# Holding the second DMA ring and the DMA transposes behind DVE writes, and reordering the first key products, at the head of a gated attention and MLP kernel

## The chip, the cores and the metric

The kernel runs on one core of one Trainium2 chip. The metric is the device time of one execution in microseconds (us). A run counts as slow when it is over 1.5% above the fastest run of the same kernel. The span of a profile is about 1.8 us shorter than the measured time.

PE is the matrix engine, DVE the vector engine, ACT the scalar engine, POOL the general engine, and SP the engine that issues most DMAs. PEld in a profile is PE's loading of weights. A DMA is a transfer from memory; a ring is the queue of DMA commands of the engine that issues them (here SP or ACT); a load lands when its last part has arrived.

## The reference

```python
def ref(A_x, A_wqkv, A_wo, B_w1, B_b1, B_w2, B_b2, gate_w):      # cut
    x = A_x                                    # 1 x 2048 x 512, bf16
    g = sigmoid((x * gate_w).sum(-1, keepdims=True))
    q, k, v = split_heads(x @ A_wqkv)          # 32 heads of 16
    phi = lambda t: where(t > 0, t + 1, exp(t)) + 1e-6
    kv  = einsum("bhsd,bhse->bhde", phi(k), v)
    z   = einsum("bhsd->bhd", phi(k))
    a   = normalized(phi(q) @ kv, phi(q) @ z) @ A_wo
    h   = layernorm(x)
    b   = (gelu(h^T @ B_w1 + B_b1) @ B_w2 + B_b2)^T
    return g * a + (1 - g) * b
```

Only the key stage matters here: k = x Wk, phi(k), the Gram product x^T phi(k), and the statistics of the layer norm, which run on DVE beside it.

## The kernel before

x is cut into 16 tiles of 128 rows. Wk has four chunks of 128 rows, Wk0 to Wk3. A key product of a tile takes four matmuls, one per chunk, and needs x transposed. Tiles 0 to 3 are transposed on PE and copied out by DVE or ACT. Tiles 4 to 15 come transposed by DMA.

```python
    load_x(nc.sync, 0, 1)                       # eight first loads of 128 KB
    load_x(nc.scalar, 1, 1)                     # on two rings: SP (sync), ACT (scalar)
    load_wk(nc.sync, 0)
    load_x(nc.scalar, 2, 1)
    load_x(nc.sync, 3, 1)
    for k, q in ((1, nc.scalar), (2, nc.sync), (3, nc.scalar)):
        load_wk(q, k)
    load_xT(4, 2)                               # DMA transposes, two tiles each
    load_xT(6, 2)
    load_x(nc.sync, 4, 4)
    # ... cut: the other loads, memsets ...
    warm_up(6)                                  # six matmuls on constants
    # ... cut ...
    transpose_tile(0, False)                    # PE transposes; copy on DVE
    transpose_tile(1, True)                     # copy on ACT
    transpose_tile(2, False)
    ln_step(0)                                  # statistics on DVE
    for k in range(2):
        for t in range(HEADS - 1):
            k_part(t, (k,))                     # chunks 0 and 1 of tiles 0, 1, 2
    transpose_tile(HEADS - 1, True)             # tile 3, copy on ACT
    ln_step(1)
    for t in range(HEADS):
        k_part(t, range(2 if t < HEADS - 1 else 0, ND))
        k_phi(t)                                # exp on ACT, two instructions on DVE
    for t in range(HEADS, NT):                  # steady state
        k_part(t, range(ND))
        k_phi(t)
        g_tile(t - LAG)                         # Gram product, four tiles behind
        if t > LAG:
            ln_step(t - LN_LAG)
        # ... cut ...
```

Of the kernel before, what the change touches and what calls it, by code (L numbers as in the profile page):

```python
# [10 lines left out]
BF16 = mybir.dt.bfloat16  # L11
# [4 lines left out]
def kernel(  # L16
# [13 lines left out]
    nc = tc.nc  # L30
    P = nc.NUM_PARTITIONS
# [6 lines left out]
    S, D = X.shape  # L38
    F = B_w1.shape[1]
    NT = S // P  # L40
    ND = D // P
# [4 lines left out]
    FB = 4  # L46
# [4 lines left out]
    w1_chunks = [(j, min(FB, NF - j)) for j in range(0, NF, FB)]  # L51
# [3 lines left out]
    wqkv_view = A_wqkv.rearrange("(k p) n -> p k n", p=P)  # L55
    wo_view = A_wo.rearrange("(j p) n -> p j n", p=P)
    w1_view = B_w1.rearrange("(t p) f -> p t f", p=P)
# [3 lines left out]
    wpool = ctx.enter_context(tc.tile_pool(name="wstream", bufs=4))  # L61
# [5 lines left out]
    def keep(shape, dtype, name):  # L67
        return persist.tile(shape, dtype, name=name, tag=name)

    def bank(name, dtype=FP32):  # L70
        return ps.tile([P, SC], dtype, name=name, tag="bank")

    xs = keep([P, NT, D], BF16, "xs")
    hs = keep([P, NT, D], BF16, "hs")
    xT = keep([P, ND, S], BF16, "xT")
    wq_sb = keep([P, ND, D], BF16, "wq_sb")
    wk_sb = keep([P, ND, D], BF16, "wk_sb")
    wv_sb = keep([P, ND, D], BF16, "wv_sb")
    wo_sb = keep([P, ND, D], BF16, "wo_sb")
# [32 lines left out]
    def mm(o, lhsT, rhs, start, stop, **kw):  # L112
        nc.tensor.matmul(o, lhsT=lhsT, rhs=rhs, start=start, stop=stop, **kw)  # L113
# [14 lines left out]
    def load_x(q, t0, n):  # L128
        q.dma_start(out=xs[:, t0 : t0 + n, :], in_=x_view[:, t0 : t0 + n, :])

    def load_wk(q, k):
        q.dma_start(out=wk_sb[:, k, :], in_=wqkv_view[:, k, D : 2 * D])

    def load_xT(t0, n):
        nc.sync.dma_start(
            out=xT[:, :, t0 * P : (t0 + n) * P], in_=X[t0 * P : (t0 + n) * P, :], transpose=True
        )

    load_x(nc.sync, 0, 1)
    load_x(nc.scalar, 1, 1)  # L140
    load_wk(nc.sync, 0)
    load_x(nc.scalar, 2, 1)
    load_x(nc.sync, 3, 1)
    for k, q in ((1, nc.scalar), (2, nc.sync), (3, nc.scalar)):
        load_wk(q, k)
    load_xT(4, 2)
    load_xT(6, 2)
    load_x(nc.sync, 4, 4)
    for t0, n in ((8, 4), (12, 4)):
        load_xT(t0, n)  # L150
        load_x(nc.sync, t0, n)
    nc.sync.dma_start(out=wq_sb[:], in_=wqkv_view[:, :, 0:D])
    w1c = []
    for c, (j0, nb) in enumerate(w1_chunks):
        w = wpool.tile([P, NT, FB * P], BF16, name="w1c", tag="wc")
        w1c.append(w)
        for t0 in range(0, NT, 8) if c == 0 else (0,):
            t1 = t0 + 8 if c == 0 else NT
            nc.sync.dma_start(
                out=w[:, t0:t1, : nb * P], in_=w1_view[:, t0:t1, j0 * P : (j0 + nb) * P]  # L160
            )
        if c == 0:
            nc.sync.dma_start(out=wv_sb[:], in_=wqkv_view[:, :, 2 * D : 3 * D])
            nc.sync.dma_start(out=wo_sb[:], in_=wo_view)

    nc.vector.memset(ones_f[:], 1.0)
    nc.vector.memset(mhalf[:], -0.5)
    nc.vector.memset(Z32[:], 0.0)
    nc.gpsimd.memset(ident[:], 0.0)
    nc.gpsimd.affine_select(  # L170
        out=ident[:], in_=ident[:], compare_op=ALU.not_equal, fill=1.0, base=0,
# [5 lines left out]
        out=maskQ[:], in_=maskH[:].rearrange("p (a m) -> p m a", m=2), op=ALU.max, axis=AX.X  # L177
# [12 lines left out]
    def warm_up(n, cols=SC):  # L190
        for _ in range(n):
            mm(wps[:, :cols], warm[:, 0:P], warm[:, :cols], True, True)

    act_warm = keep([P, 1], FP32, "act_warm")
    nc.scalar.activation(out=act_warm[:], in_=ones_f[:], func=ACT.Exp)
    warm_up(6)

    def transpose_tile(t, on_act):
        pt = bank("pt", BF16)
        for k in range(ND):  # L200
            nc.tensor.transpose(pt[:, k * P : (k + 1) * P], xs[:, t, k * P : (k + 1) * P], ident[:])  # L201
        dst = xT[:, :, t * P : (t + 1) * P]
        src = pt[:].rearrange("p (k s) -> p k s", k=ND)
        if on_act:
            nc.scalar.activation(out=dst, in_=src, func=ACT.Copy)  # L205
        else:
            nc.vector.tensor_copy(out=dst, in_=src)

    def phi(dst, acc):
        e = work.tile([P, SC], BF16, name="e", tag="e", bufs=6)  # L210
        nc.scalar.activation(out=e[:], in_=acc[:], func=ACT.Exp)  # L211
        nc.vector.tensor_scalar(  # L212
            out=e[:], in0=e[:], scalar1=1.0, scalar2=PHI_EPS, op0=ALU.min, op1=ALU.add
        )
        nc.vector.scalar_tensor_tensor(  # L215
            out=dst, in0=acc[:], scalar=0.0, in1=e[:], op0=ALU.max, op1=ALU.add
        )
# [3 lines left out]
    def k_part(t, ks):  # L221
        if t not in kaccs:
            kaccs[t] = bank("kacc")
        for k in ks:
            mm(
                kaccs[t][:], xT[:, k, t * P : (t + 1) * P], wk_sb[:, k, :],
                k == 0, k == ND - 1,
            )

    def k_phi(t):  # L230
        phi(pk[:, t, :], kaccs.pop(t))
# [46 lines left out]
    def ln_step(u):  # L278
        ln_stats(u)
        if u % TPC == TPC - 1:  # L280
            ln_rstd(u // TPC)

    HEADS = 4
    transpose_tile(0, False)
    transpose_tile(1, True)
    transpose_tile(2, False)
    ln_step(0)
    for k in range(2):
        for t in range(HEADS - 1):
            k_part(t, (k,))  # L290
    transpose_tile(HEADS - 1, True)
    ln_step(1)
    for t in range(HEADS):
        k_part(t, range(2 if t < HEADS - 1 else 0, ND))
        k_phi(t)
    LAG = 4
    LN_LAG = 3
# [156 lines left out]
    for j in range(NB0, NF):  # L454
        c, jj = divmod(j, FB)
# [18 lines left out]
        out=gg[:], in0=gth[:], scalar1=0.5, scalar2=0.5, op0=ALU.mult, op1=ALU.add  # L474
    )
    nc.vector.tensor_scalar(
        out=c1[:], in0=gth[:], scalar1=-0.5, scalar2=0.5, op0=ALU.mult, op1=ALU.add
# [3 lines left out]
    for t in range(NT):  # L481
        c, tl = divmod(t, TPC)
        aps = bank("aps")
        for j in range(ND):
# [3 lines left out]
            out=a_sc[:], in_=aps[:], func=ACT.Identity,  # L488
            scale=gg[:, t : t + 1], bias=c2[:, t : t + 1],
        )  # L490
        for c0, W in ((0, D - P), (D - P, P)) if t == NT - 1 else ((0, D),):
            cs = slice(c0, c0 + W)
            yps = bank("yps")
            for f in range(NF):
# [6 lines left out]
                out=ot[:, :W], in0=yps[:, :W], scalar=c1[:, t : t + 1], in1=a_sc[:, cs],  # L501
# [35 lines left out]
```

## Time and profile before

| | before |
|---|---|
| time, first three runs | 164.32 us median (164.17 to 164.72) |
| span of the profile | 162.5 us |
| PE busy | 158.1 us, 97% |
| first key product / tile 4's first key product | 4.82 / 9.00 us |

The first view is the page of the kernel before: its span, the busy times of the engines, and the chain of work that ended last.

```profile
span 162.5 us, 2183 instructions
...
PE 158.1 (97%) x823; PEld 72.8 (45%) x837; DVE 89.5 (55%) x210; ACT 63.3 (39%) x97; POOL 17.5 (11%) x34
...
PE 97%; issue 0%; DVE 0%
```

PE is busy nearly from end to end, so only the few places where it waits can give time back. The timeline of PE shows where they are. Its columns are the start, the busy time, engine, line, operation, the tiles and their shapes, the count, and in brackets the idle time before with what ended it.

```profile
2.08 1.48 PE L113 MATMUL wps<-const-bfloat16-1.0 128*128 128x512 bf16 x3
3.55 1.47 PE L201 MATMUL pt<-ident,xs 128*128 128x128 bf16 x12
4.82 1.97 PE L113 MATMUL kacc<-wk_sb,xT 128*128 128x512 bf16 x6
6.62 0.39 PE L201 MATMUL pt<-ident,xs 128*128 128x128 bf16 x4
6.84 3.19 PE L113 MATMUL kacc<-wk_sb,xT 128*128 128x512 bf16 x14
9.86 1.03 PE L113 MATMUL gacc<-pk,xs 128*128 128x512 bf16 x4
```

A row merges instructions of one group. The rows overlap a little because the record of one such matmul lasts 0.38 us (its end is modelled), while the next one starts 0.216 us after it. The six key products (kacc) from 4.82 take until 6.62: three with Wk0, then three with Wk1, which start at 5.97. From 6.62 on the stream is dense: 10 products for tiles 0 to 3, four for tile 4 from 9.00.

ACT's timeline in the same kernel shows the order of the copies (xT) and the exps (e):

```profile
4.62 0.60 ACT L205 ACTIVATE xT<-pt 128x512 bf16<-128x512 bf16 x1 [0.42 <-PE pt L201]
7.04 0.60 ACT L205 ACTIVATE xT<-pt 128x512 bf16<-128x512 bf16 x1 [1.82 <-PE pt L201]
7.54 2.26 ACT L211 ACTIVATE e<-kacc 128x512 bf16<-128x512 f32 x4
```

The copy of tile 3 runs at 7.04, ahead of the exps, and PE wants its result only at 8.14.

### The profile page before, as it was taken

The numbers are of one execution on the slowest core, as the hardware profiler recorded it, in microseconds if no ns is written. First come the engines' busy times: TensorE is split into PE (matmuls) and PEld (weight loads), VectorE is DVE, ScalarE is ACT, GpSimd is POOL, SyncE is SP. The second block draws the span as 40 slices with busy tenths as digits, with TensorE's granted clock in tenths as the row PEclk, the third lists the DMA queues.
The fourth block names the chain that finished last, engine by engine and source line by source line (L and its number), as shares of the span: only waits on it lengthen the run. The fifth ranks groups of instructions, "written<-read, shape, count | busy, mean of one in ns | idle before, by whom it ended". The sixth has DMA issues, their size and how long they took to land.

```text
span 162.5 us, 2183 instructions
## 1 busy us (share of the span) xinstructions
PE 158.1 (97%) x823; PEld 72.8 (45%) x837; DVE 89.5 (55%) x210; ACT 63.3 (39%) x97; POOL 17.5 (11%) x34
## 2 busy tenths in 40 slices
PE   7999999999999999999999999999999999999993
PEld 3544444444444444444444444444444444444452
DVE  0599999967999999519995301166211111111112
ACT  3463386648667483212865113111122222111110
POOL 3000711200110000001415500050000000000000
PEclk9999999999999999999999999999999999999999
DMA  5999999999900006600892699822000001110001
GB/s 152 239 212 237 280 316 334 379 386 387 338 12 0 0 0 221 230 4 0 280 318 80 197 325 297 315 99 102 32 32 32 32 32 41 48 44 33 32 32 32
DMA packets 30057, 25.05 MB, mean 154 GB/s; under 512 B 7968, under 2 KB 29472, under 8 KB 30048
## 3 DMA queue, kind: packets, MB, share of 16 engines
q1 hardware_dynamic: 27744, 21.76, 43.4%
q0 software_dynamic: 1440, 2.38, 5.8%
q10 hardware_dynamic: 864, 0.79, 1.4%
q8 instruction: 6, 0.10, 0.3%
q14 instruction: 3, 0.02, 0.0%
HBM read 21.11 MB, written 2.23 MB: 144 GB/s over the span
## 4 chain that ended last, share of the span: by engine, by line
PE 97%; issue 0%; DVE 0%
PE uacc L113 30%; PE yps L113 30%; PE kacc L113 9%; PE aps L113 8%; PE gacc L113 8%; PE qacc L113 8%; PE wps L113 2%; PE pt L201 1%; PE denps L113 1%; PE kvps L113 0%; PE w2ps L113 0%; DVE ot L500 0%; PE pt L330 0%
## 5 line engine op out<-in xcount | busy, mean ns | idle before, releaser
L113 PE MATMUL uacc<-hs,w1c 128*128 128x512 bf16 x219 | 51.0, 379 | 0.4
L113 PE MATMUL yps<-uT,w2c 128*128 128x512 bf16 (+2 forms) x234 | 50.6, 366 | 0.2
L500 DVE SCALAR_TENSOR_TENSOR ot<-yps,c,a_sc 128x512 bf16<-128x512 f32 (+2 forms) x17 | 12.2, 720 | 45.2 <-PE yps L113 42.0
L113 PEld LDWEIGHTS <-w2c 128*128 128x128 bf16 x238 | 22.8, 98 | 25.9
L113 PEld LDWEIGHTS <-w1c 128*128 128x128 bf16 x224 | 21.8, 98 | 26.3 <-issue 0.2
L487 ACT ACTIVATE a_sc<-aps,c,gg 128x512 f32<-128x512 f32 x16 | 12.4, 777 | 46.7 <-PE aps L113 39.6
L324 ACT ACTIVATE uT<-uacc,bcol 128x512 bf16<-128x512 f32 x14 | 9.3, 688 | 21.7 <-PE uacc L113 21.7
L113 PE MATMUL aps<-W2sb,pqT 128*128 128x512 bf16 x63 | 16.2, 379 | 0.1
L113 PE MATMUL kacc<-wk_sb,xT 128*128 128x512 bf16 x63 | 16.2, 385 | 0.0
L113 PE MATMUL qacc<-xT,wq_sb 128*128 128x512 bf16 x63 | 16.2, 379 | 0.0
L113 PE MATMUL gacc<-pk,xs 128*128 128x512 bf16 x62 | 15.5, 379 | 0.1
L251 ACT ACTIVATE hs<-xs,nmr,rstd 128x512 bf16<-128x512 bf16 x16 | 12.8, 805 | 1.9 <-DVE nmr L245 1.9
L211 ACT ACTIVATE e<-qacc 128x512 bf16<-128x512 f32 x16 | 9.6, 597 | 9.2 <-PE qacc L113 8.3
L211 ACT ACTIVATE e<-kacc 128x512 bf16<-128x512 f32 x16 | 9.3, 595 | 6.9 <-PE kacc L113 5.6
L439 POOL DMA_DIRECT2D rex<-rd_dram x16 | 9.5, 602 | 22.9 <-DVE pqT L441 20.5
L215 DVE SCALAR_TENSOR_TENSOR pk<-kacc,e 128x512 bf16<-128x512 f32 x16 | 11.1, 692 | 0.6
L215 DVE SCALAR_TENSOR_TENSOR pqT<-qacc,e 128x512 bf16<-128x512 f32 x16 | 11.1, 692 | 0.6
L235 DVE BATCH_NORM_STATS2 stats<-xs 128x6 f32<-128x512 bf16 x16 | 10.9, 682 | 0.0
L212 DVE TENSOR_SCALAR e<-e 128x512 bf16<-128x512 bf16 x32 | 9.0, 281 | 3.3 <-ACT e L211 3.3
L426 DVE CUSTOM_DVE_ANT_0 junk<-xs,gw_b 128x512 bf16<-128x512 bf16 x16 | 9.8, 683 | 0.0
L276 DVE TENSOR_TENSOR zacc<-zacc,pk 128x512 f32<-128x512 f32 x14 | 9.6, 685 | 0.2
L113 PEld LDWEIGHTS <-xT 128*128 128x128 bf16 x64 | 6.3, 99 | 7.5 <-ACT xT L205 0.4
(61 smaller groups left out, 71.6 us busy)
## 6 DMA issues: line engine op xcount, KB each, us to landing
w2c<-in_B_w_dram SPq DMA_DIRECT2D x8, 896.0 KB, 6.2
w1c<-in_B_w_dram SPq DMA_DIRECT2D x2, 2048.0 KB, 14.0
w1c<-in_B_w_dram SPq DMA_DIRECT2D x3, 1024.0 KB, 11.6
rex<-rd_dram POOLq DMA_DIRECT2D x16, 128.0 KB, 3.5
out_dram<-ot SPq DMA_DIRECT2D x13, 128.0 KB, 1.7
xs<-in_A_x_dram SPq DMA_DIRECT2D x3, 512.0 KB, 5.2
wq_sb<-in_A_wqkv_dram SPq DMA_DIRECT2D x1, 512.0 KB, 6.1
wv_sb<-in_A_wqkv_dram SPq DMA_DIRECT2D x1, 512.0 KB, 10.6
```

What stands on the lines that cost most here:

```text
L113: nc.tensor.matmul(o, lhsT=lhsT, rhs=rhs, start=start, stop=stop, **kw)
L211: nc.scalar.activation(out=e[:], in_=acc[:], func=ACT.Exp)
L212: nc.vector.tensor_scalar(out=e[:], in0=e[:], scalar1=1.0, scalar2=PHI_EPS, op0=ALU.min, op1=ALU.add)
L215: nc.vector.scalar_tensor_tensor(out=dst, in0=acc[:], scalar=0.0, in1=e[:], op0=ALU.max, op1=ALU.add)
L235: nc.vector.bn_stats(out=stats[:], in_=xs[:, t, :])
L251: nc.scalar.activation(out=hs[:, t, :], in_=xs[:, t, :], func=ACT.Identity, scale=rstd[:, t : t + 1], bias=nmr[:, t : t + 1],)
L276: nc.vector.tensor_tensor(out=zacc[:], in0=first, in1=pk[:, t, :], op=ALU.add)
L324: nc.scalar.activation(out=uT[:, j, :], in_=acc[:], func=ACT.Gelu_apprx_tanh, bias=bcol[:, j : j + 1])
L426: nc.vector.tensor_tensor_reduce(out=junk[:], in0=xs[:, t, :], in1=gw_b[:], scale=1.0, scalar=0.0, op0=ALU.mult, op1=ALU.add, accum_out=gp ...
L439: nc.gpsimd.dma_start(out=rex[:], in_=src.unsqueeze(1).to_broadcast([8, HEAD, SC]))
L487: nc.scalar.activation(out=a_sc[:], in_=aps[:], func=ACT.Identity, scale=gg[:, t : t + 1], bias=c2[:, t : t + 1],)
L500: nc.vector.scalar_tensor_tensor(out=ot[:, :W], in0=yps[:, :W], scalar=c1[:, t : t + 1], in1=a_sc[:, cs], op0=ALU.mult, op1=ALU.add,)
```

## The change

The intent: let x0 and Wk0 arrive alone and early by holding ACT's ring back (a DVE memset into the place that x1 will fill makes ACT's first DMA wait); bring the Wk chunks ahead of x3; order the key products by the landings of their chunks; keep the DMA transposes off the DMA engines until tile 1's copy is done (a second memset into tile 4's place). The copies of tiles 0 and 1 are split so that chunk 0 comes first. One warm-up matmul less.

The diff, cut to its core (the rest moves definitions up unchanged):

```diff
+    def hold(dst):
+        nc.vector.memset(dst, 0.0)
+    # three memsets moved up
+    hold(xs[:, 1, 0:2])
     load_x(nc.sync, 0, 1)
     load_x(nc.scalar, 1, 1)
     load_wk(nc.sync, 0)
-    load_x(nc.scalar, 2, 1)
-    load_x(nc.sync, 3, 1)
-    for k, q in ((1, nc.scalar), (2, nc.sync), (3, nc.scalar)):
-        load_wk(q, k)
+    load_wk(nc.scalar, 1)
+    load_x(nc.sync, 2, 1)
+    load_wk(nc.scalar, 2)
+    load_wk(nc.sync, 3)
+    load_x(nc.scalar, 3, 1)
 ...
-    warm_up(6)
+    warm_up(5)
 ...
+    transpose_part(0, 0, 1, False)          # chunk 0, then chunks 1 to 3; copies on DVE
+    transpose_part(0, 1, ND, False)
+    transpose_part(1, 0, 1, False)
+    transpose_part(1, 1, ND, False)
+    hold(xT[:, :, 4 * P : 4 * P + 2])
     load_xT(4, 2)
     load_xT(6, 2)
 ...
-    transpose_tile(0, False)
-    transpose_tile(1, True)
-    transpose_tile(2, False)
+    for k in range(2):
+        for t in range(2):
+            k_part(t, (k,))
+    transpose_part(2, 0, ND, False)
     ln_step(0)
-    for k in range(2):
-        for t in range(HEADS - 1):
-            k_part(t, (k,))
-    transpose_tile(HEADS - 1, True)
+    for t in range(2):
+        k_part(t, (2,))
+    for t in range(2):
+        k_part(t, (3,))
+        k_phi(t)
+    transpose_part(3, 0, ND, True)          # copy on ACT, behind two exps
     ln_step(1)
-    for t in range(HEADS):
-        k_part(t, range(2 if t < HEADS - 1 else 0, ND))
+    for t in range(2, HEADS):
+        k_part(t, range(ND))
         k_phi(t)
```

More of the change, by code (lines that the diff above doesn't have):

```diff
@@ L137, in load_xT @@
         )
+    def hold(dst):
+        nc.vector.memset(dst, 0.0)
+    nc.vector.memset(ones_f[:], 1.0)
+    nc.vector.memset(mhalf[:], -0.5)
+    nc.vector.memset(Z32[:], 0.0)
+    hold(xs[:, 1, 0:2])
     load_x(nc.sync, 0, 1)
@@ L141 @@
     load_wk(nc.sync, 0)
-    load_x(nc.scalar, 2, 1)
-    load_x(nc.sync, 3, 1)
-    for k, q in ((1, nc.scalar), (2, nc.sync), (3, nc.scalar)):
-        load_wk(q, k)
-    load_xT(4, 2)
-    load_xT(6, 2)
-    load_x(nc.sync, 4, 4)
-    for t0, n in ((8, 4), (12, 4)):
-        load_xT(t0, n)
-        load_x(nc.sync, t0, n)
-    nc.sync.dma_start(out=wq_sb[:], in_=wqkv_view[:, :, 0:D])
-    w1c = []
-    for c, (j0, nb) in enumerate(w1_chunks):
-        w = wpool.tile([P, NT, FB * P], BF16, name="w1c", tag="wc")
-        w1c.append(w)
-        for t0 in range(0, NT, 8) if c == 0 else (0,):
-            t1 = t0 + 8 if c == 0 else NT
-            nc.sync.dma_start(
-                out=w[:, t0:t1, : nb * P], in_=w1_view[:, t0:t1, j0 * P : (j0 + nb) * P]
-            )
-        if c == 0:
-            nc.sync.dma_start(out=wv_sb[:], in_=wqkv_view[:, :, 2 * D : 3 * D])
-            nc.sync.dma_start(out=wo_sb[:], in_=wo_view)
-    nc.vector.memset(ones_f[:], 1.0)
-    nc.vector.memset(mhalf[:], -0.5)
-    nc.vector.memset(Z32[:], 0.0)
+    load_wk(nc.scalar, 1)
[3 more added lines that the diff above has]
+    load_x(nc.scalar, 3, 1)
     nc.gpsimd.memset(ident[:], 0.0)
@@ L195, with transpose_part @@
     nc.scalar.activation(out=act_warm[:], in_=ones_f[:], func=ACT.Exp)
-    warm_up(6)
-    def transpose_tile(t, on_act):
+    warm_up(5)
+    def transpose_part(t, k0, k1, on_act):
         pt = bank("pt", BF16)
-        for k in range(ND):
+        for k in range(k0, k1):
             nc.tensor.transpose(pt[:, k * P : (k + 1) * P], xs[:, t, k * P : (k + 1) * P], ident[:])
-        dst = xT[:, :, t * P : (t + 1) * P]
-        src = pt[:].rearrange("p (k s) -> p k s", k=ND)
+        dst = xT[:, k0:k1, t * P : (t + 1) * P]
+        src = pt[:, k0 * P : k1 * P].rearrange("p (k s) -> p k s", k=k1 - k0)
         if on_act:
@@ L283 @@
     HEADS = 4
-    transpose_tile(0, False)
-    transpose_tile(1, True)
-    transpose_tile(2, False)
-    ln_step(0)
-    for k in range(2):
-        for t in range(HEADS - 1):
-            k_part(t, (k,))
-    transpose_tile(HEADS - 1, True)
+    transpose_part(0, 0, 1, False)
[3 more added lines that the diff above has]
+    hold(xT[:, :, 4 * P : 4 * P + 2])
+    load_xT(4, 2)
+    load_xT(6, 2)
+    load_x(nc.sync, 4, 4)
+    for t0, n in ((8, 4), (12, 4)):
+        load_xT(t0, n)
+        load_x(nc.sync, t0, n)
+    nc.sync.dma_start(out=wq_sb[:], in_=wqkv_view[:, :, 0:D])
+    w1c = []
+    for c, (j0, nb) in enumerate(w1_chunks):
+        w = wpool.tile([P, NT, FB * P], BF16, name="w1c", tag="wc")
+        w1c.append(w)
+        for t0 in range(0, NT, 8) if c == 0 else (0,):
+            t1 = t0 + 8 if c == 0 else NT
+            nc.sync.dma_start(
+                out=w[:, t0:t1, : nb * P], in_=w1_view[:, t0:t1, j0 * P : (j0 + nb) * P]
+            )
+        if c == 0:
+            nc.sync.dma_start(out=wv_sb[:], in_=wqkv_view[:, :, 2 * D : 3 * D])
+            nc.sync.dma_start(out=wo_sb[:], in_=wo_view)
+    for k in range(2):
+        for t in range(2):
+            k_part(t, (k,))
+    transpose_part(2, 0, ND, False)
+    ln_step(0)
+    for t in range(2):
[4 more added lines that the diff above has]
+    transpose_part(3, 0, ND, True)
     ln_step(1)
-    for t in range(HEADS):
-        k_part(t, range(2 if t < HEADS - 1 else 0, ND))
+    for t in range(2, HEADS):
+        k_part(t, range(ND))
         k_phi(t)
```

## The prediction

> **What bounds the kernel now.** The matrix engine: the page's first part gives PE 158.1 of 162.5 us, and the chain that ended last is 97% PE. The timeline of PE shows 512-column matmuls every 0.216 us from 6.62 us to the end, almost without a break. So only the head can move: tile 4's key product starts at 9.00, and a shift of it should reach the end one for one, as later loads have slack (x transposes of tiles 8 to 11 land at 13.5, needed at 15.7; first W1 half 26.5, needed at 33.2).
>
> **The head before.** Six warm-up matmuls at 0.427 us; x0 lands at 3.50, x1 3.68, Wk0 4.16, x2 4.37, x3 5.71, Wk1 5.93, Wk2 6.45, Wk3 6.62. After 4.37 landings slow down: the DMA transposes (issued from 3.70) share the engines. PE transposes from 3.55, key products run from 4.82, with about 0.5 us of waits for the copies of tiles 1 and 2 and for Wk1 (5.97). Matmuls reach full speed at about 5.4.
>
> **The change.**
> 1. x1 leaves about 0.4 us later (DVE's held write ends at about 1.1; before 0.81). x0 should land at about 3.2, but x1 only at about 3.9: eight loads move at about 128 KB per 0.4 us whatever the ring. The Trainium skill (DMA: Bandwidth & Descriptors, "Issuing engines are not separate DMA queues") has all rings on the same 16 engines; the near joint landing of x0 and x1 agrees.
> 2. Without transposes among them, all eight loads should be there by about 6.0 instead of 6.6.
> 3. Key products start about 0.48 us after x1, at 4.4 instead of 4.8. The last chunk of tile 0 starts at X = 6.4 (estimate: 4.4, two slow products at 0.43, two half slow, tile 2's transposes 0.22, two at 0.22).
> 4. A new wait: ACT's order becomes exp of tile 0, exp of tile 1, then the copy of tile 3's transpose; before, that copy came first (7.04 to 7.64, nobody waited). The skill (TensorE: Matmul & The Clock Gate, Part 1) has ACT strictly first in, first out; the trace's ACT rows are in program order. Exps follow at 0.56 us, so the copy runs from X+1.6 to X+2.2, while PE wants tile 3 at X+1.5: a PE stall of about 0.75 us. Tile 4 then starts at about X+3.15 = 9.5. Without the stall: 8.75.
> 5. DMA transposes start when DVE has copied tile 1, about 5.0 instead of 3.70. The first pair took 3.96 us to land, so lands at about 8.8, needed at 9.3.
>
> **Sum.** Gain 0.25 us in loads and order, loss 0.75 at ACT: about +0.4 us, reduced a little for the chance that X comes sooner. Prediction 164.6 us, range 163.8 to 165.4; faster by over 2%: 1%, within 2%: 97%, slower by over 2%: 2%.
>
> **What will show it.** x1 landing after 3.8, the last of the eight loads by 6.1; first key product at 4.3 to 4.5; a gap of 0.5 to 0.9 us on PE before tile 3's key products, ended by ACT's copy; tile 4 starting at 9.2 to 9.7; the same length from there. If tile 4 starts before 9.0, step 4 is wrong.
>
> **What would make it wrong.** Earlier landings (X under 5.9) give a small gain. A later first transpose pair makes tile 4 wait. The clock: on the skill's same page about 3.4 us of activity in a free-running window opens it; with one warm-up less it may open a window later, costing up to 1.5 us. Runs of the same kernel already differ by 0.5 us.

## The result, and the profile after

The changed kernel ran at 164.72 us median (164.25 to 164.84, six runs), before at 164.40 (164.05 to 164.72, six runs of the same rounds). The ratio is 1.0016, 95% interval 0.9998 to 1.0035. A ratio here is the mean time of one kernel's fast runs over that of the other's of the same rounds, so it is not quite the ratio of the medians. Later the same kernel gave 1.0026 (1.0008 to 1.0044). With the repeat it is slower by about 0.2% (the first interval alone just includes no difference).

The page after:

```profile
span 163.1 us, 2187 instructions
...
PE 157.3 (96%) x822; PEld 72.3 (44%) x836; DVE 90.0 (55%) x215; ACT 62.8 (38%) x96; POOL 17.5 (11%) x34
...
PE 93%; DMA 2%; ACT 1%; issue 1%; DVE 0%; ACTq 0%
```

The chain now holds DMA and ACT. PE's timeline after:

```profile
2.95 1.04 PE L186 MATMUL pt<-ident,xs 128*128 128x128 bf16 x8
3.79 0.75 PE L113 MATMUL kacc<-wk_sb,xT 128*128 128x512 bf16 x2
5.55 0.59 PE L113 MATMUL kacc<-wk_sb,xT 128*128 128x512 bf16 x2 [1.02 <-DMA wk_sb<-in_A_wqkv_dram]
5.98 0.39 PE L186 MATMUL pt<-ident,xs 128*128 128x128 bf16 x4
6.21 1.02 PE L113 MATMUL kacc<-wk_sb,xT 128*128 128x512 bf16 x4
7.07 0.39 PE L186 MATMUL pt<-ident,xs 128*128 128x128 bf16 x4
7.30 1.03 PE L113 MATMUL kacc<-wk_sb,xT 128*128 128x512 bf16 x4
8.69 1.90 PE L113 MATMUL kacc<-wk_sb,xT 128*128 128x512 bf16 x8 [0.36 <-ACT xT L190]
10.43 1.03 PE L113 MATMUL gacc<-pk,xs 128*128 128x512 bf16 x4
```

and ACT's:

```profile
7.06 1.09 ACT L196 ACTIVATE e<-kacc 128x512 bf16<-128x512 f32 x2 [2.55 <-PE kacc L113]
8.03 0.60 ACT L190 ACTIVATE xT<-pt 128x512 bf16<-128x512 bf16 x1
8.51 0.62 ACT L196 ACTIVATE e<-kacc 128x512 bf16<-128x512 f32 x1
```

PE starts its key products 1.03 us earlier than before and then stands still twice: until Wk1 at 5.55, and until ACT's copy of tile 3 at 8.69. The brackets show idle time after the modelled end; counted from start to start the second gap is 0.53 us (7.945 to 8.689, less 0.216). Tile 4 starts at 9.56 instead of 9.00.

In these two traces the 0.56 us can be written out, counted from the first product with Wk1 (5.974 before, 5.553 after):

| term | us |
|---|---|
| Wk1 can be used earlier | -0.42 |
| tile 2's product with Wk0 now lies behind Wk1 | +0.22 |
| tile 2's four PE transposes now lie behind Wk1 | +0.23 |
| wait for ACT's copy of tile 3 | +0.53 |
| sum, against 0.56 measured | +0.56 |

The first term is that of two single runs. Other traces with the same order of loads and products show how far it moves: with the head of before, tile 4 started at 9.38 in experiment 10, where Wk1 landed at 6.31; with the head of the changed kernel it started at 9.45 (experiment 11) and 9.87 (experiment 12). The mean loss in the times is 0.27 us here and 0.43 us later, so the 0.56 us of this pair is not the average loss.

In every trace the last matmul of the program starts 150.5 us after tile 4's first product, plus any wait for DVE near 32 us (experiments 5, 6, 8, 10 and 11). So tile 4's start, with any such wait added, is the measure of the head.

Landings in us, read from the completion semaphores of each load (a load adds 16 steps; the landing is the last):

| kernel | x0 | x1 | Wk0 | Wk1 | x2 | Wk2 | Wk3 | x3 | tile 4 starts |
|---|---|---|---|---|---|---|---|---|---|
| before | 3.50 | 3.68 | 4.16 | 5.93 | 4.37 | 6.45 | 6.62 | 5.71 | 9.00 |
| after | 2.91 | 3.26 | 3.59 | 5.51 | 5.68 | 6.17 | 6.34 | 6.58 | 9.56 |

The first three loads came 0.4 to 0.6 us earlier, the last of the eight at the same time as before.

### The profile page after: what moved, and what is told of

It reads as the page before. It is cut to its first block, busy times and chain, and to the rows that moved or that the text cites. A ratio compares the mean times of both kernels' runs of the same rounds, so it can differ in the third digit from the quotient of the medians.

```text
span 163.1 us, 2187 instructions
## 1 busy us (share of the span) xinstructions
PE 157.3 (96%) x822; PEld 72.3 (44%) x836; DVE 90.0 (55%) x215; ACT 62.8 (38%) x96; POOL 17.5 (11%) x34
## 4 chain that ended last, share of the span: by engine, by line
PE 93%; DMA 2%; ACT 1%; issue 1%; DVE 0%; ACTq 0%
PE yps L113 30%; PE uacc L113 29%; PE qacc L113 9%; PE aps L113 8%; PE gacc L113 8%; PE kacc L113 8%; DMA wk_sb<-in_A_wqkv_dram 2%; ACT e L196 1%; PE denps L113 1%; PE kvps L113 0%; ACT xT L190 0%; ACTq L129 0%; PE w2ps L113 0%; DVE ot L513 0%; PE pt L186 0%
```

## The experiments

Twelve kernels ran; all gave correct results. Ratios are to the kernel before. One run of before took 957 us, and one of experiment 3 took 167.69 us at a granted clock of 0.989; both are slow and left out of the ratios.

### 1. Tile 3's copy on DVE

```diff
-    transpose_part(3, 0, ND, True)
+    transpose_part(3, 0, ND, False)
```

> The changed kernel, with the copy of tile 3's transpose on DVE instead of ACT; nothing else. Theory (ACT's queue order costs 0.53 us): DVE is free at about 7.65 us and copies in 0.42, so tile 3's key products follow tile 2's without a gap at about 8.16 instead of 8.69, tile 4 starts at about 9.03 instead of 9.56, and the time falls by about 0.5 us, to 0.998 to 1.000 of before. Rival (the loss is the late Wk and the transposes held back, ACT's copy only fills time that would be waited anyway): tile 4 then waits for its transposed x or for something else, still starts after 9.4, and the time stays at about 1.0016 of before.

Measured: 166.31 us, ratio 1.0116 (1.0103 to 1.0129). Both theories missed: it is about 1.6 us slower than the changed kernel. DVE's timeline of this kernel:

```profile
8.26 0.69 DVE L200 SCALAR_TENSOR_TENSOR pk<-kacc,e 128x512 bf16<-128x512 f32 x1
8.87 0.28 DVE L197 TENSOR_SCALAR e<-e 128x512 bf16<-128x512 bf16 x1
9.18 0.69 DVE L200 SCALAR_TENSOR_TENSOR pk<-kacc,e 128x512 bf16<-128x512 f32 x1
9.79 0.41 DVE L192 COPY xT<-pt 128x512 bf16<-128x512 bf16 x1
```

and PE's:

```profile
7.54 1.03 PE L113 MATMUL kacc<-wk_sb,xT 128*128 128x512 bf16 x4
10.26 1.04 PE L113 MATMUL kacc<-wk_sb,xT 128*128 128x512 bf16 x4 [1.70 <-DVE xT L192]
```

The program writes the phis of tiles 0 and 1 before this copy, and a phi is two DVE instructions as well as an exp. I had checked when DVE was free and not what stood ahead of the copy in DVE's own order. The transposes were ready at 7.70; the copy ran at 9.79, behind two phis. The gap is 1.86 us. This run shows the predicted mechanism more strongly, on another engine: the wait is the work written ahead of the copy.

### 2. Without the hold on ACT's ring

```diff
-    hold(xs[:, 1, 0:2])
```

> The changed kernel without the DVE write that holds ACT's ring back. Theory (the hold only reorders the first two loads, PE waits for Wk1 afterwards in any case): x0 lands about 0.5 us later (3.4 instead of 2.9), x1 stays within 0.4 us of 3.3, Wk1 lands within 0.3 us of 5.5, tile 4 starts within 0.3 us of 9.56; time within 0.2% of the changed kernel. Rival (the hold is what brought Wk1 forward from 5.93 to 5.51): Wk1 lands at 5.9 or later and tile 4 starts at 9.9 or later, time 0.25% longer than the changed kernel.

Measured: 164.91 us, ratio 1.0030 (1.0016 to 1.0044). x0 landed at 3.41, x1 3.60, Wk0 4.24, Wk1 4.42, x2 5.90, x3 6.76. The time is within 0.2% of the changed kernel, as the theory said, but both theories missed on Wk1: it came 1.1 us earlier without the hold, not at 5.5 or later. The hold brings three loads forward and puts the fourth back. PE did not stand still for Wk1 here: its first four products ran at half speed, 0.427 us apart, until 6.00, when x2 (5.90) was there. It waited for ACT's copy again 0.53 us. Tile 4 started at 10.09 in the profiled run, part of that because PE's clock opened only at 7.06 us there (see the clock below).

### 3. Without the hold on the DMA transposes

```diff
-    hold(xT[:, :, 4 * P : 4 * P + 2])
```

> The changed kernel without the DVE write that holds the DMA transposes back (they then leave at about 3.0, once x0 has landed, instead of 4.44). Theory of the prediction (transposes share the engines and slow the loads): Wk1 lands at 5.9 or later, the last of the eight loads after 7.0, tile 4 at 9.9 or later. Rival (the loads are slow by engines that lag, transposes or not): Wk1 within 0.2 us of 5.5, last load within 0.3 of 6.6, tile 4 within 0.2 of 9.56, and the same time.

Measured: 165.48 us (median of the five fast runs), ratio 1.0065 (1.0046 to 1.0085). The transposes were issued at 2.67, and their packets (256 bytes each; those of the eight loads are 1 KB) moved from 4.66. Wk1 landed at 5.30 (with the hold 5.51), so it came no later. But Wk2 came at 6.52 (with the hold 6.17), Wk3 at 6.99 (6.34) and x3 at 8.68 (6.58), and PE waited for x3, as PE's timeline shows:

```profile
6.56 1.07 PE L113 MATMUL kacc<-wk_sb,xT 128*128 128x512 bf16 x4 [0.35 <-DMA wk_sb<-in_A_wqkv_dram]
8.73 0.40 PE L186 MATMUL pt<-ident,xs 128*128 128x128 bf16 x4 [1.10 <-DMA xs<-in_A_x_dram]
```

Each theory is half right: the hold does not speed the loads in front, and it protects the loads issued last. (x3 was also issued 0.47 us later than in the changed kernel, at 3.00, right after x0's landing at 2.98 on the semaphore that the two then share; it still took 5.7 us to land, against 4.05.)

### 4. The kernel before, with its DMA transposes held back

```diff
     transpose_tile(0, False)
+    nc.vector.memset(xT[:, :, 4 * P : 4 * P + 2], 0.0)
+    load_xT(4, 2)                          # and the loads after it, moved here
```

> The kernel before, with only its DMA transposes held back by a DVE write behind the copy of tile 0's transpose (they leave at about 4.7 instead of 3.70). Tile 4 of before starts 3.03 us after Wk1 could be used (5.97). Theory (transposes slow the loads): Wk1 lands at about 5.4 to 5.6, tile 4 starts at 8.5 to 8.9 (bounded by the PE, which reaches Wk1 at about 5.85), time 0.1 to 0.5 us under before. Rival (lagging engines, whatever else runs): Wk1 stays at 5.8 to 6.0, tile 4 at 8.9 to 9.1, time as before or longer where tile 4's transposed x comes later than 8.8.

Measured: 164.40 us against 164.43, ratio 0.9999 (0.9987 to 1.0011). Wk1 landed at 6.33, the last of the eight at 6.74, and tile 4 started at 9.40; Wk1 and tile 4 came later than either theory said. Not one packet of a transpose moved before 6.15 us in this trace, and 15 of Wk1's 16 steps were in by 5.98. So the prediction's theory, that transposes are what slowed the loads after 4.37, falls. The load on the DMA engines does not explain the late parts either. The next view shows stretches of this trace; the last three columns are PE's granted clock, the mean busy share of the 16 DMA engines, and GB/s:

```profile
5.25:5.50 0.25, 0.25 (x2) 0.10 (x1) 0.25 (x2) 0.03 (x1) 0.00 (x0) 1.00 0.55 189
5.50:5.75 0.25, 0.25 (x3) 0.15 (x2) 0.25 (x2) 0.00 (x0) 0.00 (x0) 1.00 0.29 98
5.75:6.00 0.25, 0.25 (x2) 0.05 (x1) 0.25 (x1) 0.00 (x0) 0.00 (x0) 1.00 0.17 57
```

The engines were busy only 0.55, 0.29 and 0.17 of the time while at least three loads were still incomplete. The changed kernel shows the same (0.50 and 0.25 busy between 5.25 and 5.75 us, before its first transpose packet at 5.84). In the order of before, where x3 is issued early, no effect of the hold on the time was measured.

### 5. Tile 3's copy on ACT, written ahead of the phis

```diff
     for t in range(2):
         k_part(t, (3,))
-        k_phi(t)
     transpose_part(3, 0, ND, True)
+    for t in range(2):
+        k_phi(t)
     ln_step(1)
```

> The changed kernel with tile 3's transpose and its copy, still on ACT, written ahead of the two phis of tiles 0 and 1 (so ACT's order is copy, exp, exp; PE's order is unchanged). Theory (place in the queue is the whole of the 0.53 us): the copy runs as soon as the transposes are done, about 0.43 us after the start of tile 0's last chunk, and tile 3's key products follow tile 2's without a gap; tile 4 starts about 3.0 us after that last chunk started less 0.6, that is about 3.5 us after the first product with Wk1 (9.0 where Wk1 lands at 5.5). Time 0.3 to 0.6 us under the changed kernel, 0.998 to 1.001 of before. Rival (first e1's reading: any copy there is late because DVE and ACT are overloaded at this point): a gap of over 0.3 us stays ahead of tile 3 or of the first Gram product, and the time stays at 1.0015 or more.

Measured: 165.31 us, ratio 1.0067 (1.0033 to 1.0100). In the head the theory was exact: no gap ahead of tile 3, tile 4 at 9.11. Yet the time rose. PE's timeline shows a new wait 23 us later:

```profile
29.83 2.75 PE L113 MATMUL gacc<-pk,xs 128*128 128x512 bf16 x12
33.24 1.02 PE L113 MATMUL gacc<-pk,xs 128*128 128x512 bf16 x4 [0.66 <-DVE pk L200]
```

The last Gram product waits 0.83 us (start to start, less 0.216) for DVE's last phi. The exps started 1.0 us later here (8.07 against 7.06), behind the copy, so DVE's first phi ended at 9.72 instead of 8.71. DVE has no pause long enough to catch up: its last phi ends at 33.19 instead of 32.17, 1.0 us later. Between 8.5 and 33 us DVE idles only 1.0 us in all in the changed kernel. Neither theory of this run had named that; the rival had the time right, for another reason.

### 6. Tile 3's copy on DVE, written ahead of the phis

The diff is that of experiment 5 with `False` in place of `True`.

> As e5, but the copy is on DVE, written ahead of the two phis, where e1 had it behind them. Theory (queue order): DVE runs it right after tile 0's statistics, no gap ahead of tile 3, the 1.86 us gap of e1 is gone entirely, time within 0.1% of e5 and 0.998 to 1.001 of before. Rival (DVE is the wrong engine for it): a gap of over 0.3 us stays.

Measured: 164.27 us, ratio 0.9996 (0.9984 to 1.0008). The gaps of the changed kernel (0.53) and of experiment 1 (1.86) are both gone, as PE's twelve products in one piece show, with DVE's copy ahead of them:

```profile
7.53 2.75 PE L113 MATMUL kacc<-wk_sb,xT 128*128 128x512 bf16 x12
7.73 0.42 DVE L192 COPY xT<-pt 128x512 bf16<-128x512 bf16 x1 [0.18 <-PE pt L186]
```

Only the place in the order differs from experiment 1. The time was not within 0.1% of experiment 5, for the reason just told: here the exps are not delayed. Tile 4 started at 9.26 and not at 9.03, although Wk1 landed at 4.34, because the clock opened only at 6.82 us and six products ran at half speed. DVE's last phi ended at 32.55, and PE's last Gram group started at 32.60: PE and DVE are level.

### 7. Experiment 6 without the hold on ACT's ring

```diff
-    hold(xs[:, 1, 0:2])
```

> e6 without the hold on ACT's ring. In e2 the two loads that were second on their rings (Wk0, Wk1) had both landed by 4.42 us, against 3.59 and 5.51 with the hold. Theory (the hold brings the first three loads forward by 0.4 to 0.6 us and puts the fourth back by 1.1; the last of the eight is at 6.6 to 6.9 either way): Wk1 again by 4.6, x2 near 5.9, last load 6.6 to 6.9; from x2 on the same work as in e6 from Wk1 on less two products, so tile 4 starts at 8.8 to 9.2 and the time is within 0.15% of e6. Rival (the hold gains): e7 is 0.2% or more slower than e6.

Measured: 164.50 us, ratio 1.0012 (0.9992 to 1.0032), with Wk1 at 4.41, x2 at 5.68, the last load at 6.54 and tile 4 at 8.95 in the profiled run. The landings are close to what the theory said. Tile 4 waited 0.17 us for its own transposed x, which landed at 8.91: the hold on the transposes was in force, and DVE's copies ahead of it ran late with x0 and x1 (3.62 and 3.82). In no other trace did tile 4 wait for its transposed x. Against experiment 6 (0.9996) the intervals overlap, so whether the hold gains or not stays open; if it does, it is less than about 0.5%.

### 8. All eight loads on one ring

```diff
-    hold(xs[:, 1, 0:2])
     load_x(nc.sync, 0, 1)
-    load_x(nc.scalar, 1, 1)
+    load_x(nc.sync, 1, 1)
     # the other six likewise on nc.sync: Wk0, Wk1, x2, Wk2, Wk3, x3
```

> e6 with all eight loads on SP's ring in the order of need (x0, x1, Wk0, Wk1, x2, Wk2, Wk3, x3) and no hold on ACT. Theory (two rings whose loads interleave let late loads overtake: half of each load's parts lag by about 1 us): with one ring each load lands about 2.1 to 2.7 us after its issue at every 0.46 us: x1 3.4, Wk0 3.9, Wk1 4.4, x2 4.9, Wk3 5.8, x3 6.3, PE waits less, tile 4 starts at 8.2 to 8.7, time 0.3 to 0.7 us under before. Rival (the lag is of the engines, not of the rings): loads from the fourth on still land only at 5.5 to 6.9, x3 after 6.6, and the time is no better than e6.

Measured: 165.04 us, ratio 1.0037 (1.0025 to 1.0050). The loads came nearly one by one, at 2.87, 3.42, 3.82, 4.78, 5.13, 5.96, 6.32, the middle ones 0.2 to 0.5 us later than hoped, and the last, x3, at 7.59. Its issue was at 4.10, and its last four steps came from 7.50 on, while packets of the DMA transposes moved (from 6.06), as in experiment 3. PE waited for it and tile 4 started at 9.60. The fourth and fifth loads came 0.5 to 0.7 us earlier than in the changed kernel, but Wk1 came earlier still, at 4.34, with two rings in experiment 6, so the theory of overtaking rings is not shown. The time is no better than that of experiment 6, as the rival said.

### 9. Experiment 6 with two statistics moved into DVE's idle time

```diff
     hold(xT[:, :, 4 * P : 4 * P + 2])
+    ln_step(0)
+    ln_step(1)
 ...
     transpose_part(2, 0, ND, False)
-    ln_step(0)
 ...
     for t in range(2):
         k_phi(t)
-    ln_step(1)
```

> e6 with the statistics of tiles 0 and 1 written on DVE right after the hold on the transposes, where DVE idles in the changed kernel (4.4 to 6.4 us), instead of before and after the phis of tiles 0 and 1. In e6 the last phi of the key stage ends at 32.55 and PE starts the last Gram product at 32.60, 0.04 late. Theory (DVE's chain of phis and statistics, without a pause from the first phi to the last, is a second bound on this stage): the last phi ends 0.5 us or more before PE wants it, no gap near 32 us; time as e6 or up to 0.2 us less, 0.998 to 1.000 of before, bounded by Wk1 and the clock. Rival (DVE does not bound): the same time as e6 and the same end of the last phi.

Measured: 163.99 us, ratio 0.9978 (0.9961 to 0.9994), and 0.995 of the changed kernel (means 164.07 and 164.86 us). It has the lowest median. PE's timeline:

```profile
3.85 0.69 PE L113 MATMUL kacc<-wk_sb,xT 128*128 128x512 bf16 x2
5.30 0.59 PE L113 MATMUL kacc<-wk_sb,xT 128*128 128x512 bf16 x2 [0.76 <-DMA wk_sb<-in_A_wqkv_dram]
5.73 0.38 PE L186 MATMUL pt<-ident,xs 128*128 128x128 bf16 x4
6.01 1.02 PE L113 MATMUL kacc<-wk_sb,xT 128*128 128x512 bf16 x4
6.87 0.39 PE L186 MATMUL pt<-ident,xs 128*128 128x128 bf16 x4
7.09 2.75 PE L113 MATMUL kacc<-wk_sb,xT 128*128 128x512 bf16 x12
9.68 1.03 PE L113 MATMUL gacc<-pk,xs 128*128 128x512 bf16 x4
```

Twelve products now run in one piece from 7.09, tile 4 from 8.82. DVE's last phi ends at 31.31, 0.82 us before PE wants it. This profiled run had an early clock (3.79 us). That experiment 9 beats experiment 6 is not shown by the times, which come with overlapping intervals; the wider margin of DVE is shown by the traces.

### 10. The kernel before, with 0.86 us more work on DVE

```diff
+    ln_stats(0)                            # once more, the same result
     LAG = 4
```

> The kernel before, with tile 0's statistics computed once more on DVE (two instructions, 0.86 us) after the phi of tile 3; results unchanged. In before the last phi of the key stage ends 0.24 us ahead of its Gram product. Theory (second bound on DVE): the last Gram group waits 0.5 to 0.7 us and the time grows by as much, 1.003 to 1.0045 of before. Rival (only PE's head counts): no gap at 32 us and the time within 0.1% of before.

Measured: 165.05 us against 164.43, ratio 1.0033 (1.0017 to 1.0049). PE waits for DVE where it did not before, 0.39 us from start to start. The first line is DVE's last phi in the kernel before, the others are of this run:

```profile
31.15 0.69 DVE L215 SCALAR_TENSOR_TENSOR pk<-kacc,e 128x512 bf16<-128x512 f32 x1
32.33 0.69 DVE L215 SCALAR_TENSOR_TENSOR pk<-kacc,e 128x512 bf16<-128x512 f32 x1
29.66 3.19 PE L113 MATMUL gacc<-pk,xs 128*128 128x512 bf16 x14
33.07 1.02 PE L113 MATMUL gacc<-pk,xs 128*128 128x512 bf16 x4 [0.22 <-DVE pk L215]
```

Extra work on DVE is therefore not free in this stage. The expectation gave the margin of before as 0.24 us. That was misread: one record of the last Gram group is missing in the trace of before, and counted rightly (the group starts 23.31 us after tile 4 in the traces without a wait) it starts at 32.31, 0.46 us after the last phi (31.85). The dose should then cost 0.40 us, which lies in the interval (0.28 to 0.81 us).

### 11. The changed kernel with the same dose

The diff is that of experiment 10, on the changed kernel.

> The changed kernel with the same 0.86 us more on DVE at the same place. Its last phi ends 0.70 us ahead of its Gram product (PE is later). Theory (second bound on DVE): a wait of 0.1 to 0.3 us only, time 0.05 to 0.2% over the changed kernel beside it. Rival: 0.86 us is paid in full (0.5% over), or nothing at all.

Measured: 164.80 us, ratio 1.0022 (1.0002 to 1.0041), against 164.95 for the changed kernel beside it. In the trace the last Gram group waits 0.15 us for DVE, as the theory said. In the times no cost can be seen: the expected 0.05 to 0.2% is below what these runs resolve, and its rival's 0.5% is not there.

### 12. The changed kernel again

> The changed kernel itself, unchanged, as the yardstick for e9 and e11 on the same chip. 1.001 to 1.003 of before; tile 4 at 9.4 to 9.7, with a gap of about 0.5 us ahead of tile 3 ended by ACT's copy. Where Wk1 lands by 4.5 us, as it did in e6, tile 4 may start by 9.3.

No edit. Measured: 164.95 us, ratio 1.0026 (1.0008 to 1.0044). Wk1 landed at 5.43, the gap ahead of tile 3 was again 0.53 us, and tile 4 started at 9.87: the clock opened at 6.29 us in this run, so a few products more ran at half speed than in the first profile (3.99 us). This is 0.17 us later than the expectation's range.

## Why the prediction was right or wrong

The direction was right and the time close (164.6 predicted, 164.72 measured; a loss of about 0.4 us predicted, 0.27 and 0.43 us measured), and so was the step that carried it, number 4. That the number came so close is in part luck: the wait was smaller than predicted, the gain that should offset it was absent, and the two errors cancelled. The stated range also held the time of the kernel before, so landing in it proves little; the gap that PE showed is the better test.

- **What bounds the kernel.** Right that only tile 4's start counts for PE and that it reaches the end one for one (150.5 us from there to the last matmul in all traces). Incomplete: "later loads have slack" looked only at loads. DVE's chain of phis and statistics ended just 0.46 us before PE wanted it. Experiments 5, 6 and 10 show this second bound. In the changed kernel it had 0.70 us of margin, because PE was late, so it did not touch the result; it does limit a repair that leaves DVE's work where it is.
- **Step 1, x1 later.** Wrong in direction. It was issued 0.31 us later (1.12 against 0.81) and yet landed at 3.26, before 3.68, predicted 3.9. In before, the steps of x0 (2.83 to 3.50) and x1 (3.00 to 3.68) interleave; after, x0 is complete (2.91) before x1's first step (3.05). Why the three come sooner and the fourth 1.1 us later (experiment 2) is not settled.
- **Step 2, all eight loads by 6.0.** Wrong. The last landed at 6.58 against 6.62. The transposes were not what slowed the loads up to Wk1: without the hold Wk1 still came at 5.30 (experiment 3), and with it the loads of before still took until 6.74, with no transpose packet before 6.15 (experiment 4). They did delay the last three loads in experiment 3. In the changed kernel eight of Wk1's 16 completion steps had come by 4.15 us, but the last only at 5.51. What makes half of the parts late was not found. It was not that all 16 DMA engines were full: they were busy only 0.50 and then 0.25 of the time between 5.25 and 5.75 us.
- **Step 3, first key product 4.4, X = 6.4.** The first product came at 3.79, better than predicted. But PE then waited for Wk1 until 5.55, which the step did not have: it took Wk1 for landed in time. X became 6.64.
- **Step 4, a wait of 0.75 us at ACT.** Right in mechanism, 0.53 in size. ACT and DVE run in the order of the program, as the Trainium skill says (TensorE: Matmul & The Clock Gate, Part 1); experiment 1 shows it for DVE (1.86 us), experiment 6 takes the whole gap away by order alone. Most of the mis-sized term is the pace of the exps: 0.56 us came from a merged row (2.26 us for four, one of which had waited for PE). The single records of before start 0.48 us apart (7.54, 8.01, 8.49), and after 0.49.
- **Step 5, transposed x at 8.8.** It came at 7.97. The transposes left at 4.44 and took 3.53 us; no wait followed.
- **Sum.** Predicted -0.25 for loads and order and +0.75 for ACT, less a little. Measured in the two traces: -0.42 for Wk1, +0.44 for the work that the new order puts behind Wk1, +0.53 for ACT. So in this pair the loads and the new order were worth nothing together, and the whole loss is the copy behind the exps. That removing the gap gives its 0.53 us back in the times is shown only across calls: experiment 6 ran at 0.9996 of before, the changed kernel at 1.0016 and 1.0026.
- **The clock.** On the skill's same page a free-running window opens PE's clock after about 3.4 us of activity. In the 14 traces (their record of the granted clock) it opened between 3.8 and 7.1 us, a range of about one such window, and it was not seen to follow the kernel: the changed kernel itself had 3.99 in one run and 6.29 in another. It adds noise to single profiles.

## What to carry to other kernels

When instructions are reordered to follow their data, write down every engine's resulting order and what stands ahead of each small copy, not only of the matmuls: here 0.53 us of waiting came from two exps ahead of one copy, and one attempted repair made it 1.86 us by putting two phis ahead. Before valuing a gain at the head of a stage, find the margin of the second engine in that stage: a gain of PE beyond DVE's 0.46 us of margin, without an earlier end of DVE's own chain, would only have become a wait at the stage's end. Count the work that remains after the last load that PE waits for; moving work behind that load can cost as much as the earlier landing gains (here 0.44 against 0.42 us).

## What the Trainium skill lacked or had wrong

- DMA: Bandwidth & Descriptors ("Issuing engines are not separate DMA queues") says that the rings share the engines, and these traces fit that: the last of the eight loads landed at 6.3 to 7.0 us in all seven traces of two-ring kernels with both holds and Wk ahead of x3, at 6.5 to 6.8 in the two without the hold on ACT's ring, and at 6.6 to 7.1 in the three in the order of before. It lacks that holding one ring back changes which load is late: Wk1 at 4.41 and 4.42 without the hold, 5.14 to 5.73 with it in all traces but one (4.34). It also lacks how far the parts of one 128 KB load can drift apart: Wk1's eighth step at 4.15 us, its last at 5.51, with the 16 engines only 0.50 busy from 5.25 to 5.50.
- The same page ("Rules for kernel authors") says that "A transpose next to ordinary DMAs needs nothing". That is about correct data; the page lacks the price in time. A 128 KB load issued behind the transposes took 5.7 us to land (one trace, experiment 3), against 4.05 with the transposes held back.
- TensorE: Matmul & The Clock Gate (Part 1) agrees with these traces on the free-running window (opening at 3.8 to 7.1 us) and on products 0.427 and 0.216 us apart. It lacks a hint for reading such profiles: the mean granted clock given for the profiled runs was 0.998 to 1.000, although the matmuls ran at half speed until 3.8 to 7.1 us.
